# Clearing semaphores in two steps, another split of the last columns, and a shorter loop body in a one-core decode kernel

## The chip, the cores and the metric

The kernel runs on one core of a Trainium2 chip. The metric is the device time of one execution in microseconds. Most executions agree within 0.3%; the times shown are medians of several runs.

## What is computed

One token of 1024 values goes through two branches whose results are added to it: attention over the last 4096 positions of a cache (32 query heads, 4 key and value heads of 128), and a gelu MLP of width 3584. Weights, caches and the output are bfloat16.

```python
xn = layernorm(x)                                   # x: (1, 1, 1024)
q = (xn @ wq).reshape(1, 1, 32, 128)                # wq: 1024 x 4096
scores = q . k[-4096:] * 128 ** -0.5                # each k head serves 8 q heads
o = softmax(scores) @ v[-4096:]
a = o.reshape(1, 1, 4096) @ wo                      # wo: 4096 x 1024
h = gelu(layernorm(xn) @ w1 + b1)                   # w1: 1024 x 3584
b = h @ w2 + b2                                     # w2: 3584 x 1024
out = x + a + b
```

## The kernel before

All weights and both caches, about 40 MB, are read once through one transfer queue that SyncE feeds. Four buffers of 4 MB (`slot[0]` to `slot[3]`) hold what is in use; a buffer gets its next content when its last reader is done. The order of the transfers is: k, wq, w1, v, w2, the first half of wo (two transfers into slot 0), the second half of wo (five transfers into slot 2, where v was: 8, 4, 2, 1 and 1 rows of 1024 values per partition, `cuts`), and at the end two output transfers of 512 values, one issued by SyncE and one by ScalarE.

The order on each engine is the order in which the program lists the operations. `Plan` records them with what they read and write; `Plan.emit` works out the waits, gives each engine one counting semaphore and each transfer one of its own, and writes the instructions out. VectorE's and TensorE's instructions stand in blocks of their own behind a branch (L109), closed by a branch that is never taken back (L116). Behind the last operation GpSimd waits for the landing of both output transfers (L103) and clears all semaphores that were used, so that the next execution finds them at zero (L104). `clear_and_free_semaphores` makes one DRAIN and one range-clear instruction for each run of neighbouring semaphore numbers. The numbers are given out in the order of allocation: 5 for the four k transfers and the one of x, then the 5 engine counts, then 23 for the transfers in program order, the two output transfers last.

The value product runs on TensorE (L475 to L477): step 0, a register-driven loop over steps 1 to 30 (`v_loop`, `UV` steps a pass, L469), and step 31. Each step is a weight load of 128 columns of the exponentials and a matmul of 512 columns of v. Each step in the loop also works out its addresses in registers (L460), each pass adds one to the counter (L471) and branches (L472). Behind step 31:

- SyncE issues the five transfers of wo's second half (L201 from L483).
- VectorE, when it is through its first ten `running` rows of w2 (L447), normalizes and gathers the heads: `o_m` (L485), `o_f` (L487), `o_bf` (L489); then it takes the other rows of w2.
- TensorE takes four rows of w2 (eight matmuls, `PE_ROWS[0]`), spreads `o_bf` over the partitions (L511), takes eight more rows of w2, and then the rows of wo.

The last eight rows of wo, c from 24 (`NB`), go to an accumulator of their own in two parts: columns 0 to `NA` of each half of the output in `acc_a`, columns `NA` to 512 in `acc_b`. For each row TensorE streams the wide part for both halves, then the narrow part for both. VectorE's running sum enters the same accumulator through four fp32 matmuls behind row 27 (L541). VectorE casts `acc_a` to bfloat16 (L544) and ScalarE `acc_b` (L545); both output transfers wait for both casts.

## Time and profile before

| | us |
|---|---|
| median of 3 runs | 101.56 |
| lowest and highest | 101.46, 101.63 |
| the profiled execution's own time | 101.56 |
| its span, first to last instruction | 99.5 |
| busy: TensorE matmuls | 47.0 |
| busy: VectorE | 68.3 |
| busy: ScalarE | 30.7 |
| busy: GpSimd | 9.1 |

The busy times are shares of different stretches, so none of them says by itself what sets the end. In the profile's rows PE is TensorE's matmuls, PEld its weight loads, DVE is VectorE, ACT is ScalarE, POOL is GpSimd, SP is SyncE; a q behind the name (POOLq, SPq, PEldq) marks an instruction of the engine's sequencer, which waits, branches, clears or issues a transfer and isn't counted as busy. A row of the timeline begins with the start and the duration in us; xN stands for N instructions merged; in brackets is the idle time before and what ended it. A row of one source line gives shortest, median and longest duration in ns, then the first and the last start in us. A row of the groups gives busy us and the mean ns of one. In the page's part 2 each digit is a fortieth of the span.

### The profile page before, as it was taken

How to read it: one execution, taken by the hardware profiler on the slowest of the kernel's cores; microseconds unless marked ns; L12 is line 12 of the kernel's file. 1: busy time of each engine (PE TensorE's matmuls, PEld its weight loads, DVE VectorE, ACT ScalarE, POOL GpSimd, SP SyncE). 2: the span in 40 equal slices, each digit the busy share in tenths (PEclk: the TensorE clock that was granted, in tenths of full speed). 3: DMA queues.
4: the chain of work that ended last, by engine and by line, in shares of the span. 5: the costliest groups of instructions: out<-in, count | busy, mean ns of one | idle time of the engine just before them, and what ended most of it. 6: DMA issues, size and time to landing. Idle time of an engine off the chain costs nothing.

```text
span 99.5 us, 819 instructions
## 1 busy us (share of the span) xinstructions
PE 47.0 (47%) x331; PEld 12.5 (13%) x199; DVE 68.3 (69%) x73; ACT 30.7 (31%) x29; POOL 9.1 (9%) x20
## 2 busy tenths in 40 slices
PE   0023200005800660002996807988911999594791
PEld 0012200001100100001111302323200111120130
DVE  0053589999999999996026687999994999400221
ACT  0050000699998999930001652000000000000001
POOL 0072190000000770000000000000000000000000
PEclk9999999999999999555599995799999589999999
DMA  7599999999999899989799999999989999999950
GB/s 205 224 421 421 421 421 421 448 461 461 474 448 414 380 403 484 403 380 530 324 428 425 421 407 433 464 435 412 518 380 388 428 421 428 421 435 412 406 217 7
DMA packets 2978, 39.90 MB, mean 401 GB/s; under 512 B 408, under 2 KB 414, under 8 KB 928
## 3 DMA queue, kind: packets, MB, share of 16 engines
q1 hardware_dynamic: 2926, 39.86, 94.8%
q8 instruction: 2, 0.03, 0.1%
q10 hardware_dynamic: 50, 0.00, 0.0%
HBM read 39.86 MB, written 0.00 MB: 400 GB/s over the span
## 4 chain that ended last, share of the span: by engine, by line
DMA 74%; PE 16%; SPq 2%; issue 1%; DVE 0%
DMA slot<-in_A_wq_dram 28%; DMA slot<-in_A_wo_dram 23%; DMA slot<-in_A_v_cache_dram 23%; PE qo_ps L460 10%; PE acc L215 5%; SPq L201 2%; PE acc L221 1%; DVE res L544 0%
## 5 line engine op out<-in xcount | busy, mean ns | idle before, releaser
L327 ACT COPY kT<-slot 32x1024 bf16<-32x1024 bf16 (+1 forms) x18 | 23.9, 1327 | 12.1 <-DVE slot L322 11.9
L447 DVE SCALAR_TENSOR_TENSOR run<-slot,hTf,run 128x1024 f32<-128x1024 bf16 x15 | 18.2, 1280 | 1.6 <-DMA slot<-in_B_w_dram 1.4
L322 DVE STREAM_TRANSPOSE slot<-slot 128x4096 bf16<-128x4096 bf16 x4 | 17.4, 4413 | 0.0
L215 PE MATMUL acc<-slot,xnT 128*1 128x512 bf16 x64 | 6.9, 608 | 18.0 <-DMA slot<-in_A_wq_dram 18.0
L331 DVE COPY kT<-slot 32x4096 bf16<-32x4096 bf16 x10 | 14.0, 1403 | 0.2
L460 PE MATMUL qo_ps<-slot,eTb 128*128 (+1 forms) x32 | 9.6, 436 | 4.0 <-DMA slot<-in_A_v_cache_dram 3.2
L215 PE MATMUL sc_ps<-slot,o 128*1 128x512 bf16 x48 | 9.1, 379 | 2.5 <-DMA slot<-in_A_wo_dram 2.5
L215 PE MATMUL sc_ps<-slot,hT 128*1 128x512 bf16 x24 | 7.1, 455 | 1.1 <-DMA slot<-in_B_w_dram 1.1
L525 DVE TENSOR_TENSOR run<-sc_ps,run 33x512 f32<-33x512 f32 x2 | 1.3, 679 | 8.1 <-PE sc_ps L215 8.1
L545 ACT CAST res<-acc 33x192 bf16<-33x192 f32 x1 | 0.3, 312 | 21.0 <-PE acc L215 21.0
L215 PE MATMUL sc_ps<-kT,qm 128*32 128x512 bf16 x32 | 5.1, 830 | 0.5 <-DVE qm L378 0.5
L513 ACT CAST o<-misc 128x32 bf16<-128x32 f32 x1 | 0.2, 185 | 15.9 <-PE misc L221 15.9
L221 PE MATMUL qo_ps<-selq,q_sb 128*128 128x4 bf16 x8 | 0.4, 169 | 9.6 <-DVE q_sb L350 9.6
L460 PEld LDWEIGHTS qo_ps<-slot,eTb 128*128 (+1 forms) x32 | 3.4, 106 | 10.0 <-issue 4.4
L314 POOL TENSOR_TENSOR run<-x,b2x 1x1024 f32<-1x1024 bf16 x1 | 2.5, 2497 | 18.4 <-DMA b2x<-in_B_b_dram 18.4
L393 DVE COPY sc<-sc_ps 128x512 f32<-128x512 f32 x1 | 0.7, 691 | 4.8 <-PE sc_ps L215 4.8
L207 PEld LDWEIGHTS <-xnT 128*1 128x1 bf16 x32 | 1.0, 121 | 22.8 <-issue 22.8
L207 PEld LDWEIGHTS <-o 128*1 128x1 bf16 x40 | 2.4, 84 | 11.9 <-issue 11.3
L236 DVE MEMSET mhalf<- 128x1 f32 x1 | 0.1, 59 | 5.3 <-PEq L191 5.3
L215 PE MATMUL acc<-slot,yT 128*1 128x448 bf16 x64 | 3.4, 353 | 0.0
L221 PE MATMUL misc<-x,spread 32*128 32x8 bf16 x4 | 0.3, 168 | 6.5 <-POOL spread L242 6.5
L392 ACT COPY sc<-sc_ps 128x512 f32<-128x512 f32 x1 | 0.6, 585 | 8.9 <-PE sc_ps L215 8.9
(84 smaller groups left out, 44.8 us busy)
## 6 DMA issues: line engine op xcount, KB each, us to landing
slot<-in_B_w_dram SPq DMA_DIRECT2D x3, 3584.0 KB, 19.0
slot<-in_A_wq_dram SPq DMA_DIRECT2D x2, 4096.0 KB, 23.0
slot<-in_A_wo_dram SPq DMA_DIRECT2D x3, 2048.0 KB, 25.1
slot<-in_A_k_cache_dram SPq DMA_DIRECT2D x4, 1024.0 KB, 8.3
slot<-in_A_v_cache_dram SPq DMA_DIRECT2D x1, 2048.0 KB, 18.6
slot<-in_A_v_cache_dram SPq DMA_DIRECT2D x2, 1024.0 KB, 21.6
slot<-in_B_w_dram SPq DMA_DIRECT2D x1, 2048.0 KB, 22.5
slot<-in_B_w_dram SPq DMA_DIRECT2D x1, 1024.0 KB, 18.1
```

The lines of the kernel that those rows point to most:

```text
L201: plan.add(eng, lambda: q.dma_start(out=out_ap, in_=in_ap), r, w, True, over)
L207: return pe.add_instruction(mybir.InstLdweights(name=nc.get_next_instruction_name(), engine=i.engine, tile_size=(P, 32), tile_position=pos ...
L215: return pe.add_instruction(mybir.InstMatmult(name=nc.get_next_instruction_name(), engine=i.engine, start_tensor_calc=start, stop_tensor_c ...
L221: op("pe", lambda: pe.matmul(out_ap, lhsT=w_ap, rhs=x_ap, start=start, stop=stop, tile_position=pos), r, w)
L314: op("pool", lambda: pool.tensor_tensor(out=run[0][0:1, :], in0=x2, in1=b2x, op=ALU.add), ("x2", "b2x"), ("run0",))
L322: op("dve", lambda s=s: dve.transpose(out=scr[:, s, :], in_=k2[:, s, :]), ("k0", "k1", "k2", "k3", "slot0"), (f"scr{s}",))
L327: op("act", lambda s0=s0, s1=s1, R=R, Cd=Cd: act.copy(out=kT[32 * Cd:32 * Cd + 32, R, s0:s1, :].rearrange("p s (c j) -> p (s c) j", j=32), ...
L331: op("dve", lambda R=R, Cd=Cd: dve.tensor_copy(out=kT[32 * Cd:32 * Cd + 32, R, :, :].rearrange("p s (c j) -> p (s c) j", j=32), in_=T3[32 ...
L393: op("dve", lambda: dve.tensor_copy(out=sc[:, 0:512], in_=sc_ps[:, 0, :]), ("sc0",), ("scs0",))
L447: op("dve", lambda: dve.scalar_tensor_tensor(out=t, in0=wap, scalar=hTf[:, c:c + 1], in1=t, op0=ALU.mult, op1=ALU.add), (key, "hTf", f"run ...
L460: return pe.matmul(qo_ps, lhsT=cols, rhs=v4[:, :, c, :], start=first, stop=last)
L525: op("dve", lambda half=half: dve.tensor_tensor(out=run[0][0:33, 512 * half:512 * half + 512], in0=bulk[:, half, :], in1=run[0][0:33, 512 ...
```

## The change

Three edits.

1. In `Plan.emit` the semaphores are allocated in another order and cleared in two steps. Allocated first are TensorE's, GpSimd's and SyncE's counts, then VectorE's and ScalarE's counts and the semaphores of the two output transfers, then those of all other transfers. GpSimd now first waits for the last counts of VectorE and ScalarE, clears 29 semaphores in two ranges of 8 and 21 numbers, then waits for the two output transfers and clears a range of 4.
2. `NA` goes from 320 to 288: VectorE casts 288 columns and ScalarE 224.
3. `UV` goes from 5 to 2: V's loop has 15 passes of two steps where it had 6 passes of five.

The line numbers behind the first edit rise by 11.

```diff
-        sems = {e: nc.alloc_semaphore(f"{e}_count") for e in self.engines}
-        used = list(sems.values())
+        sems = {e: nc.alloc_semaphore(f"{e}_count") for e in ("pe", "pool", "sp")}
+        used, ends = list(sems.values()), []
         value, ticks = {}, {e: 0 for e in self.engines}
+        for e in ("dve", "act"):
+            sems[e] = nc.alloc_semaphore(f"{e}_count")
+            ends.append(sems[e])
+        for n in done:
+            value[n] = (nc.alloc_semaphore(f"dma{n}"), 16)
+            ends.append(value[n][0])
         for n, (eng, fn, r, w, dma, _) in enumerate(ops):
             if dma is not None:
+                if n in done:
+                    continue
                 value[n] = (nc.alloc_semaphore(f"dma{n}") if dma is True else dma, 16)
                 used.append(value[n][0])
             elif n in wanted:
@@
             if o[0] not in ("dve", "pe"):
                 put(n)
+        for e in ("dve", "act"):
+            nc.gpsimd.wait_ge(sems[e], ticks[e])
+        nc.clear_and_free_semaphores(used)
         for s, v in [value[m] for m in done]:
             nc.gpsimd.wait_ge(s, v)
-        nc.clear_and_free_semaphores(used)
+        nc.clear_and_free_semaphores(ends)
@@
-    NA = 320
+    NA = 288
     NB = 24
-    UV = 5
+    UV = 2
```

## The prediction

> **What bounds the kernel now.** I read the page first, its parts 2 to 4, to see which engine or queue the end hangs on; then the timeline of the last stretch and the rows of the clearing lines; last the V loop, since the third edit lies there.

> ```profile
> span 99.5 us, 819 instructions
> PEclk9999999999999999555599995799999589999999
> DMA  7599999999999899989799999999989999999950
> q8 instruction: 2, 0.03, 0.1%
> q1 hardware_dynamic: 2926, 39.86, 94.8%
> DMA 74%; PE 16%; SPq 2%; issue 1%; DVE 0%
> ```

> Queue q1 alone fills 94.8% of all 16 DMA engines' time and the chain that ended last is DMA for 74% of the span. From about slice 3 to slice 37 the transfers run without a hole, so what engines do in between counts only if it keeps q1 from having work. What lies behind the last weight transfer is not covered by DMA:

> ```profile
> 97.11 0.24 PE L215 MATMUL acc<-slot,o 128*1 128x192 bf16 x2
> 96.98 0.31 PE acc L215 x2
> 97.32 0.48 DVE L544 CAST res<-acc 33x320 bf16<-33x320 f32 x1 [2.17 <-PE acc L215]
> 97.40 0.31 ACT L545 CAST res<-acc 33x192 bf16<-33x192 f32 x1 [21.02 <-PE acc L215]
> 97.87 0.27 SPq L201 DMA_DIRECT2D out_dram<-res  x1
> 97.89 0.48 ACTq L201 DMA_DIRECT2D out_dram<-res  x1
> L103 POOLq EVENT_SEMAPHORE  x1: 17/17/17, 99.0 to 99.0; - x1
> L104 POOLq DRAIN  x1: 98/98/98, 99.2 to 99.2; - x1
> L104 POOLq EVENT_SEMAPHORE_RANGE_CLEAR  x1: 222/222/222, 99.3 to 99.3; - x1
> ```

> The tail is serial: the last matmuls start at 96.98; VectorE's cast ends at 97.80, ScalarE's at 97.71; both output transfers, which wait for both casts, are issued at 97.87 and 97.89; GpSimd's wait for the second landing ends with a DRAIN from 99.2 to 99.3, and a range clear of 222 ns is the last instruction of all. The span is 99.5 and this execution's own time 101.56, so some 2 us lie outside the span; I carry them over unchanged. The median of the runs is 101.56 too, so the sum needs no correction.

> **Edit 1, the clear in two steps.** Before, one clear of all 33 semaphores (5 from the head of the kernel, 5 engine counts, 23 transfers) stands behind the landing. After, GpSimd waits for the last VectorE and ScalarE counts, clears 29 semaphores in two ranges (8 and 21), each with its own DRAIN, then waits for the two landings and clears a range of 4 with a third DRAIN.

> The first step starts when the casts end, about 97.8, and costs two drains of 98 ns, two clears that share at most 222 ns if the time goes by the count (2 × 222 if it doesn't), and a wait of 17: 0.44 to 0.66 us, so done by 98.3 to 98.5. The landing comes at 99.2. It hides behind the output's flight with 0.7 us to spare; were that cover gone it would cost its whole 0.44 to 0.66. Nothing is queued behind the new waits on GpSimd but the old ones: its last other instruction in the program is the memset of L418, which ScalarE's and VectorE's last work does not need. The third DRAIN and the wait are the ones that stood there before.

> What falls off the path is the difference between clearing 33 and clearing 4. A clear of 4 is not in the trace.

> ```profile
> L242 POOLq MOVE  x1: 29/29/29, 5.6 to 5.6; - x1
> ```

> From below: 17 ns, the semaphore wait of L103, so a gain of 0.205. From above: 222 ns, if the instruction's time does not depend on the count, a gain of nothing. A one-register instruction of the same sequencer takes 29 ns; with that as the fixed part and the other 193 ns shared by 33 semaphores, 4 take 29 + 4 × 5.8 = 52 ns. I take 52, **a gain of 0.17 us**, since 222 ns is far above any other single instruction of that sequencer that does not wait, which speaks for a walk over the range.

> **Edit 2, 288 to 224.** Both casts read PSUM with 33 partitions. The price of a column comes from the same engines' casts and copies out of PSUM at other widths:

> ```profile
> L393 DVE COPY sc<-sc_ps 128x512 f32<-128x512 f32 x1 | 0.7, 691 | 4.8 <-PE sc_ps L215 4.8
> L544 DVE CAST res<-acc 33x320 bf16<-33x320 f32 x1 | 0.5, 482 | 2.2 <-PE acc L215 2.2
> L392 ACT COPY sc<-sc_ps 128x512 f32<-128x512 f32 x1 | 0.6, 585 | 8.9 <-PE sc_ps L215 8.9
> L545 ACT CAST res<-acc 33x192 bf16<-33x192 f32 x1 | 0.3, 312 | 21.0 <-PE acc L215 21.0
> L513 ACT CAST o<-misc 128x32 bf16<-128x32 f32 x1 | 0.2, 185 | 15.9 <-PE misc L221 15.9
> ```

> VectorE: (691 − 482) / 192 = 1.09 ns a column, so 32 fewer save 35 ns: 447. ScalarE: (312 − 185) / 160 = 0.79, or (585 − 312) / 320 = 0.85 ns, so 32 more cost 25 to 27: 338. TensorE streams the same 512 columns a half; only the point between the parts moves. The wide part's last matmuls start at 96.98 and the narrow part's at 97.11 by their rows, so 320 columns take some 0.135 us, 0.42 ns each, and VectorE starts 32 × 0.42 = 13 ns earlier, ScalarE when it did. VectorE then ends at 97.32 − 0.013 + 0.447 = 97.75, ScalarE at 97.40 + 0.338 = 97.74. VectorE is still last, by about 10 ns. The issues move by 97.80 − 97.75: **a gain of 0.05 us**, bounds 0.03 (ScalarE turns out last, at 1.09 ns a column) and 0.06. It is nothing if the weights' last landing sets more than the matmuls; it doesn't, since the casts are in series behind it.

> **Edit 3, two V steps a pass.**

> ```profile
> 65.66 1.40 PE L460 MATMUL qo_ps<-slot,eTb 128*128 x5 [0.27 <-issue]
> 67.33 1.40 PE L460 MATMUL qo_ps<-slot,eTb 128*128 x5 [0.27 <-issue]
> 68.99 1.65 PE L460 MATMUL qo_ps<-slot,eTb 128*128 x6 [0.27 <-issue]
> L460 PE MATMUL qo_ps<-slot,eTb x32: 376/379/634, 60.3 to 70.3; 128*128 x30, 128*128 128x512 bf16 x2
> L460 PEldq FUSED_REGOPS  x30: 51/74/79, 60.5 to 69.8; - x30
> L460 PEldq ALU_OP  x24: 32/32/42, 60.8 to 69.9; - x24
> L472 PEldq COMPARE_BRANCH  x6: 79/229/257, 61.8 to 70.1; - x6
> ```

> A pass of five steps repeats after 67.33 − 65.66 = 1.67 us. Its matmuls fill 1.40, the last of them 0.38 long, so the five starts are (1.40 − 0.38) / 4 = 0.255 apart, and from the last start to the next pass's first lie 1.67 − 1.02 = 0.65: register work and a taken branch of 229 ns. A pass of two takes 0.255 + 0.65 = 0.90. Fifteen of them are 13.6 us against six of 1.67, 10.0: **TensorE ends V about 3.5 us later**, at 74.2 where it was 70.6. If the loop's overhead were wholly hidden it would be nothing later. What waits for that:

> ```profile
> 70.57 1.89 PE L215 MATMUL sc_ps<-slot,hT 128*1 128x512 bf16 x8
> 70.67 2.23 SPq L201 DMA_DIRECT2D slot<-in_A_wo_dram  x5
> 73.88 0.67 DVE L485 TENSOR_TENSOR o_m<-qo_ps,grs 32x512 f32<-32x512 f32 x1
> 75.90 0.26 PE L221 MATMUL misc<-o_bf,spread 32*128 32x32 bf16 x4 [3.44 <-DVE o_bf L489]
> 77.23 7.26 DVE L447 SCALAR_TENSOR_TENSOR run<-slot,hTf,run 128x1024 f32<-128x1024 bf16 x6 [1.39 <-DMA slot<-in_B_w_dram]
> 77.25 5.17 PE L215 MATMUL sc_ps<-slot,hT 128*1 128x512 bf16 x16 [1.09 <-DMA slot<-in_B_w_dram]
> 87.04 1.24 PE L215 MATMUL sc_ps<-slot,o 128*1 128x512 bf16 x5 [1.17 <-DMA slot<-in_A_wo_dram]
> ```

> SyncE's five transfers of wo's second half, 2.23 us of issuing, move to 74.2 to 76.5. At that time q1 still holds the rest of w2, which lands at 77.2, and wo's first half, whose second part lands at 87.0; the queue can't run dry. VectorE's o_m slips by 0.3 (73.88 to 74.2) and is made good by the 1.39 it idles before w2 at 77.23; TensorE's eight rows move to 74.2 to 76.1, into the 3.44 it idled before o_bf, now due at 76.2. All three meet the old schedule at 77.2. So this edit costs nothing, by a cover of some 1 us on VectorE and TensorE and over 10 us on SyncE; on the path it would cost the whole 3.5.

> [...]

> **Sum.** 101.56 − 0.17 − 0.05 = **101.34 us**, 0.2% less.

> **The rivals.** *The clear does not shorten* (its time is fixed, or GpSimd is not the last to finish outside the span): only edit 2 is left, 101.51. For it: no row shows a short clear. Against it: 222 ns beside 17 and 29.

> *TensorE's code is fetched late*: the slower side. The loop's body loses three steps of four instructions (register operation, addition, weight load, matmul), so all that follows lies 12 instructions earlier.

> ```profile
> L116 PEldq COMPARE_BRANCH  x1: 79/79/79, 97.0 to 97.0; - x1
> GB/s 0 0 0 0 0 0 0 0 0 0 0 298 0 0 0 0 0 0 0 0 0 19 19 0 0 0 0 0 0 0 0 0 0 0 0 0 0 0 0 0
> q8 instruction: 1, 0.02, 3.4%
> ```

> These are the closing branch and the DMA view of 97.4 to 99.6 (40 slices of 0.055 us). TensorE's program is by far the longest, so I take the code for its. One of the two code transfers starts in slice 11, at 98.0, 1.0 us behind TensorE's closing branch, and takes 3.4% of 16 engines' 2.2 us, 1.2 us of one. Now it is hidden: GpSimd ends later. If it is asked for when TensorE runs over the end of what it holds, and the 12 instructions push that point behind the wait for the other engines, then it decides: 1.0 + 1.2 us begin only when GpSimd has ended, 101.34 + 2.2 = 103.5. Against it: 1.0 us fits a fetch set off by the branch itself, which the edit leaves where it stands in time. [...]

> *The cover of the V loop fails*: a pass costs over 0.25 us more than worked out, or slower rows on TensorE use up the 1.2 us it idles at 87: half a microsecond, 101.8. *More than the sum*: TensorE's clock is half in the slice at 77 (PEclk 5), behind an idle stretch that now closes; if a faster TensorE brought the last rows forward it would gain some 0.2 more, 101.1. The last rows wait for DMA, so hardly.

> **How the numbers follow.** Forecast 0.62, the clear that does not shorten 0.12, late code 0.13, failed cover 0.05, more than the sum 0.08. The likeliest own range is 101.2 to 101.5 by the bounds of the two gains (0.03 to 0.27, so 101.29 to 101.53) and the 0.17 between the runs shown. The range of 101.1 to 101.8 takes in every case but late code. 0.2% of 101.56 is 0.20 us, about what a measurement of this kernel can tell from no change, and it goes through the middle of the forecast: of its 0.62 I count 0.40 beyond and 0.22 within. Faster 0.40 + 0.08 = 0.48; same 0.22 + 0.12 = 0.34; slower 0.18.

> **What would show it.** Right: a last range clear of about 50 ns, two clears before 98.6, casts of about 447 and 338 ns that end together, output issues at about 97.82, V's end near 74, and VectorE and TensorE both starting on w2 at 77.2. Wrong: a last clear near 222 ns; a code transfer that starts behind GpSimd's end, which would show as a short span and a long time; a last weight landing later than 97.0.

## The result, and the profile after

| | before | after |
|---|---|---|
| median, 22 runs each | 101.80 us | 101.39 us |
| lowest | 101.46 us | 100.97 us |
| highest | 102.54 us | 102.26 us |
| ratio | | 0.9949 (95% interval 0.9929 to 0.9970) |
| the profiled execution's own time | 101.56 us | 101.63 us |
| its span | 99.5 us | 99.8 us |

The changed kernel is 0.5% faster, 0.52 us by the ratio (0.31 to 0.72) and 0.41 by the medians. The ratios here and below, and the medians of spans and of what lies outside them, count the executions within 1.5% of the fastest of the same kernel. The two profiled executions don't show it: the one of after is longer, by its time and by its span. Where its span went is seen in the first microseconds of the timeline, before any edit can act:

```profile
0.80 3.81 SPq L192 DMA_DIRECT2D slot<-in_A_k_cache_dram  x4
33.74 2.72 PE L226 MATMUL acc<-slot,xnT 128*1 128x512 bf16 x24 [6.14 <-DMA slot<-in_A_wq_dram]
```

The four k transfers take 3.81 us to issue (3.22 in the profile of before), and TensorE gets wq 0.6 us later than there (33.74; 33.13 before). This lateness stays up to the last weight. It isn't the kernel's: a second profile of the same changed kernel (g1_again below) has 3.20. Spans of the 22 runs go from 99.2 to 100.0, so single executions can't be subtracted; only stretches of a trace that begin at the same event can, and medians over runs.

The tail of after, timeline and the rows of the clearing lines (L111 is the wait for the casts, L112 the early clears, L114 the wait for the landings, L115 the late clear):

```profile
97.87 0.45 DVE L555 CAST res<-acc 33x288 bf16<-33x288 f32 x1 [2.15 <-PE acc L226]
97.97 0.34 ACT L556 CAST res<-acc 33x224 bf16<-33x224 f32 x1 [20.09 <-PE acc L226]
98.40 0.27 SPq L212 DMA_DIRECT2D out_dram<-res  x1
98.41 0.48 ACTq L212 DMA_DIRECT2D out_dram<-res  x1
L111 POOLq EVENT_SEMAPHORE  x1: 17/17/17, 98.3 to 98.3; - x1
L112 POOLq DRAIN  x2: 66/77/88, 98.4 to 98.6; - x2
L112 POOLq EVENT_SEMAPHORE_RANGE_CLEAR  x2: 74/113/152, 98.5 to 98.7; - x2
L114 POOLq EVENT_SEMAPHORE  x1: 17/17/17, 99.5 to 99.5; - x1
L115 POOLq DRAIN  x1: 55/55/55, 99.7 to 99.7; - x1
L115 POOLq EVENT_SEMAPHORE_RANGE_CLEAR  x1: 47/47/47, 99.8 to 99.8; - x1
```

The late clear takes 47 ns where one of 222 stood, and the DRAIN ahead of it 55 where 98 stood. The early clears are over by 98.9, while the output is still on its way (the wait for its landing ends at 99.5). The two casts end together, at 98.32 and 98.31. Next the V loop and what waits for it:

```profile
71.49 0.64 PE L471 MATMUL qo_ps<-slot,eTb 128*128 x2 [0.31 <-issue]
72.39 0.64 PE L471 MATMUL qo_ps<-slot,eTb 128*128 x2 [0.27 <-issue]
73.34 0.64 PE L471 MATMUL qo_ps<-slot,eTb 128*128 x2 [0.31 <-issue]
74.25 0.94 PE L471 MATMUL qo_ps<-slot,eTb 128*128 x3 [0.27 <-issue]
77.81 7.27 DVE L458 SCALAR_TENSOR_TENSOR run<-slot,hTf,run 128x1024 f32<-128x1024 bf16 x6 [0.47 <-DMA slot<-in_B_w_dram]
77.83 3.61 PE L226 MATMUL sc_ps<-slot,hT 128*1 128x512 bf16 x16 [0.17 <-DMA slot<-in_B_w_dram]
82.73 3.61 PE L226 MATMUL sc_ps<-slot,o 128*1 128x512 bf16 x16 [1.28 <-DMA slot<-in_A_wo_dram]
```

A pass lasts 0.93 on average ((74.25 − 71.49) / 3 = 0.92 here), V ends at 75.2, and both engines still wait for w2: VectorE 0.47 us, TensorE 0.17. The page's third part lacks something:

```profile
q1 hardware_dynamic: 2926, 39.86, 94.3%
q8 instruction: 1, 0.02, 0.1%
```

There is one code transfer, not two; the one that stood at 98.0 is gone (the DMA view from 97.8 on lists none). The span shows no gain from that, but the time that lies outside the span got shorter. Each run has a time and a span, and their difference is far steadier than either: over the 22 runs of after its median is 1.80 us, and over 34 runs of the kernel before, taken with the first experiments below, 2.11. This difference holds what comes before the first recorded instruction and what comes after the last; it doesn't say which of the two changed. **Some 0.3 us of the gain are there**, where the prediction carried "some 2 us" over unchanged.

### The profile page after: what moved, and what is told of

Same layout as the page of the kernel before. It is cut to its first block, busy times and chain, and to the rows that moved or that the text cites. A ratio compares the mean times of both kernels' runs of the same rounds, so it can differ in the third digit from the quotient of the medians.

```text
span 99.8 us, 842 instructions
## 1 busy us (share of the span) xinstructions
PE 48.5 (49%) x331; PEld 12.1 (12%) x199; DVE 68.3 (68%) x73; ACT 30.7 (31%) x29; POOL 8.7 (9%) x20
## 3 DMA queue, kind: packets, MB, share of 16 engines
q1 hardware_dynamic: 2926, 39.86, 94.3%
HBM read 39.86 MB, written 0.00 MB: 399 GB/s over the span
## 4 chain that ended last, share of the span: by engine, by line
DVE 40%; PE 23%; DMA 19%; issue 6%; POOL 2%; ACT 2%; SPq 0%; DVEq 0%; POOLq 0%
DMA slot<-in_A_wo_dram 19%; DVE slot L333 16%; DVE kT L342 13%; PE qo_ps L471 11%; PE sc_ps L226 6%; PE misc L232 2%; PE acc L226 2%; DVE sel L313 2%; ACT e L426 1%; DVE eTb L430 1%; DVE m_loc L411 1%; DVE h_pre L440 1%; PE acc L232 1%; DVE q_sb L361 1%; POOL spread L253 1%
## 5 line engine op out<-in xcount | busy, mean ns | idle before, releaser
L471 PE MATMUL qo_ps<-slot,eTb 128*128 (+1 forms) x32 | 11.4, 436 | 5.3 <-issue 3.0
L226 PE MATMUL sc_ps<-kT,qm 128*32 128x512 bf16 x32 | 5.9, 957 | 0.5 <-DVE qm L389 0.5
L226 PE MATMUL sc_ps<-slot,hT 128*1 128x512 bf16 x24 | 5.5, 379 | 0.2 <-DMA slot<-in_B_w_dram 0.2
L524 ACT CAST o<-misc 128x32 bf16<-128x32 f32 x1 | 0.2, 186 | 15.9 <-PE misc L232 15.9
```

The lines of the kernel that those rows point to most:

```text
L226: return pe.add_instruction(mybir.InstMatmult(name=nc.get_next_instruction_name(), engine=i.engine, start_tensor_calc=start, stop_tensor_c ...
L471: return pe.matmul(qo_ps, lhsT=cols, rhs=v4[:, :, c, :], start=first, stop=last)
```

## The experiments

Each names its edit against the kernel it starts from. "Outside" is the median over its runs of time less span (spans are known to 0.1 us); the runs of the kernel before on the same chip gave 2.10 to 2.12 in every group.

### One edit at a time

```diff
e1_clear: Plan.emit of after; NA = 320, UV = 5
e2_cols: before with NA = 288
e3_loop: before with UV = 2
e4_clear_cols: after with UV = 5
```

> The clear in two steps alone (320 columns, five V steps a pass). Theory A, the gain is the serial tail and adds up by edits: the last DRAIN takes 55 ns (98 before) and the last range clear 47 ns (222 before), so landing to end of span is 0.22 us shorter and the ratio is 0.9978. Theory B, the shorter loop carries what exceeds the sum: here as in A, 0.9978. Theory C, the new order of the semaphores or the early instructions move something ahead of the tail as well: ratio at or below 0.996, and the last wo landing earlier than in the kernel before measured on the same chip.

> 288 to 224 alone. All theories: casts of 449 and 340 ns that end within 20 ns of each other, the output transfers issued 0.85 us after the last matmuls start, 0.05 us less than the 0.89 before; ratio 0.9995. It can't be told from no change by the time, only by those rows.

> Two V steps a pass alone. Theory A: V ends some 4 us later, all that waits for it meets the old schedule at w2's landing, ratio 1.000 (within 0.002). Theory B: the loop carries the excess, ratio 0.997 or lower. Both expect one code transfer in place of two, since it was so with all three edits.

> The clear and the columns with five V steps a pass, that is, the changed kernel without the loop edit. Theory A: 0.27 us less than before, ratio 0.9973, as with the loop edit. Theory B: 0.998 or higher, so that the loop edit is needed for the rest. Two code transfers, the second at about 98 us, as before.

| | ratio (95% interval) | median span | outside |
|---|---|---|---|
| before | 1 | 99.6 | 2.11 |
| e1_clear | 0.9977 (0.9947 to 1.0007) | 99.35 | 2.13 |
| e2_cols | 1.0008 (0.9976 to 1.0041) | 99.45 | 2.12 |
| e3_loop | 0.9975 (0.9955 to 0.9995) | 99.65 | 1.83 |
| e4_clear_cols | 1.0019 (0.9988 to 1.0049) | 99.55 | 2.11 |

The clear shortens the span and leaves the outside alone; the loop does the reverse. Theory C, something ahead of the tail, has no sign: e1_clear's ratio is what its tail gives. Theory B, that the loop carries part of the gain, is borne out by the outside column and by the ratio of e3_loop, whose interval leaves out theory A's 1.000 (0.9975 is a little above the 0.997 that B asked for). Theory A is right about the tails, which e3_loop leaves as they were:

```profile
L104 POOLq DRAIN  x1: 98/98/98, 99.3 to 99.3; - x1
L104 POOLq EVENT_SEMAPHORE_RANGE_CLEAR  x1: 222/222/222, 99.4 to 99.4; - x1
```

while e4_clear_cols has the rows of after:

```profile
L115 POOLq DRAIN  x1: 55/55/55, 99.6 to 99.6; - x1
L115 POOLq EVENT_SEMAPHORE_RANGE_CLEAR  x1: 47/47/47, 99.7 to 99.7; - x1
```

The time of e4_clear_cols is a miss for theory A: 0.9973 was expected, its interval begins at 0.9988. Its rows show the shorter tail, but its median span is only 0.05 below that of before, and three of its twelve runs have 2.9 to 3.5 us outside the span, which two of 34 runs of before have (above 3); why is not known. Spans scatter by more than the tail's gain, so it takes many runs to see it in them: over all 98 runs, here and below, with the changed kernel's clear (g3_one left out, whose end moves for another reason) the mean span is 99.49, over the 131 with one clear at the end 99.68. That is 0.18 us less (0.12 to 0.25 by resampling the runs), where the rows give 0.22 for the clear and 0.04 for the columns, which most of the 98 have too. The columns alone show in the rows only:

```profile
96.87 0.30 PE acc L215 x2
97.19 0.45 DVE L544 CAST res<-acc 33x288 bf16<-33x288 f32 x1 [2.17 <-PE acc L215]
97.29 0.34 ACT L545 CAST res<-acc 33x224 bf16<-33x224 f32 x1 [20.23 <-PE acc L215]
97.72 0.27 SPq L201 DMA_DIRECT2D out_dram<-res  x1
```

From the last matmuls' start (chain of waits) to the output's issue are 97.72 − 96.87 = 0.85 us; before, 97.87 − 96.98 = 0.89.

### Is it the length of TensorE's program or the pace of its loop?

```diff
f1_pad (from after; 12 more instructions)
+    for _ in range(12):
+        ldw(ocol(0), (0, 0), ("o8",))
     bulk_rows(list(range(16)), wo_row, ocol, "o8")
f2_short (from before; 12 fewer)
-    bulk_rows(list(range(16)), wo_row, ocol, "o8")
+    bulk_rows(list(range(4, 16)), wo_row, ocol, "o8")
f3_three (from after)
-    UV = 2
+    UV = 3
g4_pad8: f1_pad with range(8)
```

f2_short leaves four rows of wo out of the result.

> The changed kernel with 12 more weight loads on TensorE ahead of wo's first row, where it idles 1.28 us before the transfer: the program is as long again as with five steps a pass, the V loop stays at two. Theory L (the length of TensorE's program sets the time outside the span): time less span goes from a median of 1.80 back to 2.1, span as changed, two code transfers again. Theory P (the pace of the V loop, and with it what TensorE does afterwards, sets it): time less span stays 1.8.

> The kernel before without the first four rows of wo on TensorE (12 instructions fewer; these rows are left out of the output), with five V steps a pass. Theory L: time less span falls from 2.11 to 1.8, one code transfer, ratio 0.997. Theory P: time less span stays 2.1, ratio 1.000, since TensorE waits for wo's transfers at the end either way.

> The changed kernel with three V steps a pass, four instructions more than with two, eight fewer than with five. [...] V ends near 73, span as changed. Theory P: between 1.8 and 2.1, about 1.9.

> The changed kernel with 8 more weight loads ahead of wo's first row: where between 4 more (three steps, 1.83) and 12 more (2.16) the time outside the span jumps. [...] If the time outside grew with each instruction, about 2.0.

| | instructions against after | outside | ratio (95% interval) |
|---|---|---|---|
| after, measured again (g1_again) | 0 | 1.79 | 0.9933 (0.9898 to 0.9968) |
| f3_three | +4 | 1.83 | 0.9949 (0.9911 to 0.9988) |
| f3_three again (g2_three) | +4 | 1.83 | 0.9943 (0.9908 to 0.9979) |
| g4_pad8 | +8 | 1.78 | 0.9939 (0.9904 to 0.9973) |
| f1_pad | +12 | 2.17 | 0.9988 (0.9943 to 1.0033) |
| f2_short (five steps) | 0 | 1.81 | 0.9967 (0.9934 to 1.0000) |

g3_one, described below, has four instructions fewer than after and 1.82.

Theory L holds in both directions. Twelve weight loads, put where TensorE waits for wo anyway, bring 2.1 back with the short loop; twelve instructions fewer give 1.8 with the long one. Between +8 and +12 the time jumps, from 1.78 to 2.17 us; from −4 to +8 it does not grow (1.82, 1.79, 1.83, 1.78). So it is a step and not a price for each instruction; what makes the step is not shown. The kernel before stands at +12, so it was beyond the step by at most four instructions.

The code transfer itself is a poorer witness. The pages of before, e2_cols, e4_clear_cols and f4_early5 have two and all kernels with the short program have one, but e1_clear and f1_pad, whose outside is that of a long program, have one as well:

```profile
q8 instruction: 1, 0.02, 0.1%
```

(the page of f1_pad, where two were expected). A page counts the transfers inside the span alone, but records can go on behind it. There e1_clear and f1_pad have no second transfer either; whether it is missing from the records or came later still is not known. g3_one, with the shortest program of all, has one (its DMA view of 100.2 to 104, in slices of 0.095 us):

```profile
GB/s 0 0 0 0 0 0 0 0 0 0 0 0 0 0 0 0 0 0 0 172 0 0 0 0 0 0 0 0 0 0 0 0 0 0 0 0 0 0 0 0
q8 instruction: 1, 0.02, 2.1%
```

It starts at 102.0, 1.9 us behind the last recorded instruction (span 100.1), in an execution of 103.0 us, which has 2.9 us outside its span. So a kernel with a short program can have such a transfer too, and late. It is the only traced execution of those near 3 us; whether all of them wait for late code is not shown. That the length of the program decides between 1.8 and 2.1 is shown; that the 0.3 us are a wait for this transfer is not.

> The changed kernel itself on the chip and in the rounds of the next three. Time less span 1.8, median span 0.2 us under that of the kernel before, ratio 0.995.

> The changed kernel with three V steps a pass. If nothing but the length of the code and the tail count, the same as two steps within the spread: ratio 0.995. If the shorter time seen before (0.9949, median 101.03) comes from V's earlier end, at or below 0.993 and below the run with two steps by 0.2% or more.

The changed kernel measured again has the expected ratio and the expected time outside the span, but not the span 0.2 us shorter: its median is 99.6, as before. With three steps V ends 1.8 us earlier than with two (72.7 against 74.5 in these two profiles) and the time is the same. The lower median of f3_three's first ten runs, 101.03, did not come again (101.41). No version tried beats the changed kernel beyond the spread.

### What the DRAIN and the clear cost

```diff
f4_early5 (from before)
+        early = [s for s in used if s.name[0] in "kx"]
+        for e in ("dve", "act"):
+            nc.gpsimd.wait_ge(sems[e], ticks[e])
+        nc.clear_and_free_semaphores(early)
         for s, v in [value[m] for m in done]:
             nc.gpsimd.wait_ge(s, v)
-        nc.clear_and_free_semaphores(used)
+        nc.clear_and_free_semaphores([s for s in used if s not in early])
```

> The kernel before with a first clear of 5 semaphores (the k transfers and x) behind the casts, the other 28 cleared behind the landings. If a clear costs a fixed part and a part by the count, as 47, 74, 152 and 222 ns for 4, 8, 21 and 33 say (23 ns and 6.0 each), the late clear takes 192 ns and the early one 54. If the late DRAIN is short because a DRAIN stood shortly before, it takes 55 ns in place of 98; if it is short because little was left to clear, 98. Ratio 0.9995 or 0.9993, which the time can't tell.

```profile
L105 POOLq DRAIN  x1: 64/64/64, 97.7 to 97.7; - x1
L105 POOLq EVENT_SEMAPHORE_RANGE_CLEAR  x1: 69/69/69, 97.8 to 97.8; - x1
L108 POOLq DRAIN  x1: 95/95/95, 99.1 to 99.1; - x1
L108 POOLq EVENT_SEMAPHORE_RANGE_CLEAR  x1: 178/178/178, 99.2 to 99.2; - x1
```

The late DRAIN takes 95 ns although another stood before it: not its history but the range behind it goes with its length (55, 64, 66, 88, 95 and 98 ns ahead of clears of 4, 5, 8, 21, 28 and 33). The clears are not linear in the count, and 192 and 54 were wrong. Groups of four fit: 1, 2, 2, 6, 7 and 9 groups give 47, 69, 74, 152, 178 and 222 ns, which 25 + 22 a group meets within 6 ns. Ratio 0.9992 (0.9958 to 1.0026), no verdict by time.

### Overdrawing the V loop's cover

```diff
g3_one (from after)
-    UV = 2
+    UV = 1
```

> The changed kernel with one V step a pass, the cover of the V loop overdrawn. A pass takes 0.65, so V ends near 80.5, 3 us behind the landing of w2 at which all met before. VectorE has 8 us of idle time left before the last sum, TensorE three waits of 1.28 us: by its rows TensorE ends the rows before the sum some 1.1 us late, at 95.5, and the end moves by 0.3 to 1.0 us: ratio 0.998 to 1.005, with time less span still 1.8. If the cover were larger than worked out, 0.995.

```profile
80.27 2.30 PE L226 MATMUL sc_ps<-slot,hT 128*1 128x512 bf16 x8
80.37 2.23 SPq L212 DMA_DIRECT2D slot<-in_A_wo_dram  x5
80.38 0.68 DVE L496 TENSOR_TENSOR o_m<-qo_ps,grs 32x512 f32<-32x512 f32 x1 [6.13 <-PE qo_ps L471]
94.98 1.28 DVE L536 TENSOR_TENSOR run<-sc_ps,run 33x512 f32<-33x512 f32 x2 [4.19 <-PE sc_ps L226]
98.16 0.45 DVE L555 CAST res<-acc 33x288 bf16<-33x288 f32 x1 [1.90 <-PE acc L226]
```

V ends at 80.3 as worked out. VectorE idles 6.13 us for it, TensorE no longer waits for wo anywhere, and the sum that needs its rows starts at 94.98. The ratio is 1.0046 (0.9994 to 1.0098): 1.1% above the changed kernel's 0.9933 in the same rounds, while time less span stays at 1.82. It rests on six of ten runs. Their median span is 100.2, 0.6 us above the changed kernel's; over all ten it is 101.0, and the median time 103.01, more than the forecast of 0.3 to 1.0 us. So the cover is real and ends somewhere between V's end at 75 and at 80. In the traced execution TensorE has no wait for DMA left behind V, so its own rows set the end there; what the longer executions wait for isn't traced.

## Why the prediction was right, and where it was off

The forecast was 101.34 us with a gain of 0.22; the median is 101.39. That the two lie so close is luck: the three first runs put the kernel before at 101.56, 22 runs put it at 101.80, and the missed 0.3 us made up for these 0.24. The gain itself was about twice the forecast, which lies below the measured interval of 0.31 to 0.72.

- *Edit 1, 0.17 us*: right, 222 − 47 = 0.175 (52 forecast for the short clear). A fixed part and a part that grows with the range was the right form; the price by the single semaphore was not, since 5 and 28 fit groups of four (69 and 178 ns), and for 4 both come out near 50. Not priced: the DRAIN, said to be "the ones that stood there before", got 0.043 shorter. The early clears are hidden behind the output's flight as said.
- *Edit 2, 0.05 us*: right, 0.04 by e2_cols' rows, too little for the times to show; casts of 449 and 340 ns against 447 and 338, VectorE last by some 10 ns.
- *Edit 3, nothing*: right for all that is in the span. V's end came 3.9 us later (forecast 3.5; a pass 0.93, not 0.90), and w2's landing took it up with 0.47 and 0.17 us to spare. The clock went as thought in these two traces: TensorE idled 0.40 us before it spread `o_bf` and 0.17 before w2 (3.44 and 1.09 in before), and had a granted clock of 1.00 from 77.8 to 81.5 where before had 0.69 from 77.2 to 82.4; 16 matmuls took 3.61 us in place of 5.17, and the 1.28 us of waiting for wo that follows swallows it. That the idle time sets the clock is not shown by more than this pair.
- *The missed term*: "I carry them over unchanged". The prediction did see that the program gets 12 instructions shorter, and that a code transfer sits at the end; it held this against the change, as late code at 103.5. The suspicion was right and the sign wrong: the shorter program saves 0.3 us outside the span. Such a saving was nowhere among the cases, since "now it is hidden" was read off the span alone. With the measured 0.3 put in afterwards: 0.175 + 0.043 + 0.04 + 0.3 = 0.56, against 0.52 measured.
- *Late code*: the reading that the transfer at 98.0 is set off by TensorE's closing branch 1.0 us earlier is weaker than it looked. In e2_cols it is 1.0 us too, in e4_clear_cols 1.4 (branch at 97.4, transfer at 98.8). The 103.5 us of this case did not come as a median; the traced execution of g3_one, with its transfer at 102.0, looks like it.
- The program's length can be counted in the traces, with the loop's body once: 494 recorded instructions of TensorE in after (634 less 14 repeats of a body of 10), 502 in g4_pad8, 506 in f1_pad and in before (616 less 5 repeats of 22). So the step lies between 502 and 506 of them; what makes it, no run here shows.

## What to carry to other kernels

In this kernel the last clear is serial with everything, so clear what is idle while the output is on its way and leave four semaphores or fewer (a clear of 4 took 47 ns, of 5 took 69, of 33 took 222). Compare time less span over runs, not spans alone: here a cost outside the recorded instructions moved with the length of a program, and at most four instructions decided over 0.39 us (1.78 with 8 more than after, 2.17 with 12). Before adding a gain to a baseline, measure the baseline in more than three runs. A loop may be rolled tighter as long as what waits for it meets another wait first; the profile of before gives that margin in the idle times.
